# Masked attention weights: transposed by one DMA in place of TensorE and ScalarE

## The chip, the cores and the metric

The kernel runs on 1 core of a Trainium2 chip. The metric is the device time of one execution in microseconds; before the change its median over 3 runs is 1413.26 us (1412.77 to 1415.63). The engines are called as the profile calls them: PE (TensorE, matmuls; PEld its weight loads), DVE (VectorE), ACT (ScalarE), POOL (GpSimd) and SP (SyncE, which here only issues DMAs).

## The reference

Attention over 8 batches of 8 heads, 576 rows of 64 columns, in which each query row keeps its 32 largest scores, followed by an MLP with a squared ReLU over the 4608 rows of 512 columns:

```python
scores = scale * np.matmul(q, k.transpose(0, 1, 3, 2))
kth = np.partition(scores, -top_k, axis=-1)[..., -top_k:-top_k + 1]   # top_k = 32
scores = np.where(scores >= kth, scores, -1e9)
attn = softmax(scores)
x = (attn @ v), heads side by side: [4608, 512]
out = np.maximum(x @ w_in, 0) ** 2 @ w_out                            # 512 -> 2048 -> 512
```

## The kernel before

The 4608 rows are 36 tiles of 128 (`NT`); of each nine, one joins the last 64 rows of two batches (`parts`). A step `n` handles one tile and one half of its heads, four heads (`G`), so there are 72 steps (`NG`). The order of instructions on every engine is that of the Python program (`manual_schedule`); semaphores between the engines come from the tiles that they read and write.

In step `n`:

- DVE selects: `select_a(n)` (L237 to L250) folds each row's 576 scores and takes the first 8 maxima, `select_b(n)` (L263 to L267) takes three more rounds of 8, and `masks(n)` (L278) makes the weights of the four heads: a score at or over the 32nd maximum keeps its exponential, any other becomes 0. The result `p` is bf16, 128 x 576 a head.
- ACT makes the exponentials `e` of this step in two pairs (`exps`, L256), in the third and the fourth of the step's four slots (`for j in range(G)`, L423).
- PE makes the scores of step `n + 1` (`qk_pair`, L221, in slots 0 and 2), which ACT copies to `s` (L226), and finishes the attention of step `n - 1`: in each slot `p_transpose(n - 1, j)` (L288) transposes one head's weights in five blocks into the PSUM tile `tp`, ACT copies it to SBUF as `pt` in two pieces (L290, L291), and `av(n - 1, j)` (L302) multiplies it with `v`.
- One item of the MLP of earlier rows stands between them in each slot (`todo`): four matmuls into `hp` (L342) with ACT's ReLU and square (L345, L346), or four matmuls into `op` (L355), the fourth of which is followed by ACT's copy (L359) and the store (L361).
- The q, k and v tiles of a later batch are loaded by SP (L190), one a slot, and used four slots later: q and k are transposed by PE into `tp` (L200) and copied by ACT (L202), v is cast by POOL (L196). In the first nine steps the MLP's weights come in the same way, one piece a slot, cast by POOL (L391).

`tp` is one PSUM buffer; the transposes of the weights, of q and k, and of the normalised tile `x` (`norm`, L328, every second step) all take it in turn. `p` has two buffers, `pt` three, `s` two.

At the end (L428) the rest of the MLP's items is spread over the last slots. Then `flags` are reduced (L458); a general path, not taken here, would follow where a fold had dropped a maximum.

Of the kernel before, what the change touches and what calls it, by code (L numbers as in the profile page):

```python
# [14 lines left out]
bf16 = mybir.dt.bfloat16  # L15
i32 = mybir.dt.int32
Act = mybir.ActivationFunctionType
# [112 lines left out]
def kernel(  # L130
# [9 lines left out]
    nc = tc.nc  # L140
    B, H, S, D = q.shape
# [4 lines left out]
    G = 4  # L146
    NG = NT * 2
# [7 lines left out]
    with ExitStack() as main:  # L155
        cst = main.enter_context(tc.tile_pool(name="cst", bufs=1))
        sb = main.enter_context(tc.tile_pool(name="sb", bufs=1))
        psp = main.enter_context(tc.tile_pool(name="psp", bufs=1, space=PSUM))
# [3 lines left out]
        idb = cst.tile([128, 128], bf16, name="idb")  # L162
# [5 lines left out]
        def parts(t):  # L168
            b0, r = 2 * (t // 9), t % 9
            if r < 4:  # L170
                return [(b0, r * 128, 128, 0)]
            if r == 4:
                return [(b0, 512, 64, 0), (b0 + 1, 512, 64, 64)]
            return [(b0 + 1, (r - 5) * 128, 128, 0)]
# [34 lines left out]
        s_t, p_t, e_t, sums_t, av_t, xT_t = {}, {}, {}, {}, {}, {}  # L209
# [60 lines left out]

        def masks(n):
            t, hg = n // 2, n % 2
            p_t[n] = sb.tile([128, G, S], bf16, name="p", bufs=2)
            if hg == 0:
                sums_t[t] = sb.tile([128, 8], f32, name="sums", bufs=2)
            for j in range(G):
                h = hg * G + j
                nc.vector.scalar_tensor_tensor(out=p_t[n][:, j, :], in0=s_t[n][:, j, :],  # L278
                                               scalar=m8_t[n][0][:, 3, j, 7:8], in1=e_t[n][:, j, :],
                                               op0=Alu.is_ge, op1=Alu.mult, accum_out=sums_t[t][:, h:h + 1])  # L280

        pt_t = {}

        def p_transpose(n, j):
            tp = psp.tile([128, 5, 128], bf16, name="tp")
            for c in range(5):
                kn = 128 if c < 4 else 64
                nc.tensor.transpose(tp[:kn, c, :], p_t[n][:, j, c * 128:c * 128 + kn], idb[:, :])  # L288
            pt = sb.tile([128, 5, 128], bf16, name="pt", bufs=3)
            nc.scalar.activation(pt[:, :4, :], tp[:, :4, :], Act.Copy)  # L290
            nc.scalar.activation(pt[:64, 4, :], tp[:64, 4, :], Act.Copy)  # L291
            pt_t[n, j] = pt

        def av(n, j):
            t, h = n // 2, (n % 2) * G + j
            if h == 0:
                av_t[t] = psp.tile([128, 8, 64], f32, name="av")
            pt = pt_t.pop((n, j))
            for (b, q0, ql, p0) in parts(t):
                for c in range(5):  # L300
                    kn = 128 if c < 4 else 64
                    nc.tensor.matmul(out=av_t[t][p0:p0 + ql, h, :], lhsT=pt[:kn, c, p0:p0 + ql],  # L302
                                     rhs=vb[b][:kn, c, h * 64:(h + 1) * 64], start=(c == 0), stop=(c == 4))


# [101 lines left out]

        begin = {1: 0}
        for b in range(2, 8):
            begin[b] = (9 * (b // 2 - 1) + 5) * 2 if b % 2 == 0 else 18 * (b // 2)  # L410
        begin_step = {}
        for b, st in begin.items():
            begin_step.setdefault(st, []).append(b)
# [2 lines left out]
        for n in range(NG + 2):  # L416
            for b in begin_step.get(n, []):
                loads += start_load(b)
            if n >= 3 and n % 2 == 1:
                norm((n - 3) // 2)  # L420
            if n < NG:
                select_a(n)
            for j in range(G):  # L423
                if 1 <= n <= NG:
                    p_transpose(n - 1, j)
                if n + 1 < NG and j in (0, 2):
                    qk_pair(n + 1, j // 2)
                take = 1 if n < NG - 2 else -(-len(todo) // max(1, (NG + 1 - n) * G - j)) if n >= NG else -(-len(todo) // max(1, (NG - n) * G - j))  # L428
                for _ in range(take):
                    if todo:  # L430
                        todo.pop(0)()
                if 1 <= n <= NG:
                    av(n - 1, j)
                if n < NG:
                    if j == 2:
                        exps(n, 0)
                        exps(n, 1)
                    if j == 3:
                        exps(n, 2)
                        exps(n, 3)  # L440
                if inflight:
                    inflight.pop(0)()
                while loads and len(inflight) < 4:
                    inflight.append(loads.pop(0)())
                if n < 9 and wq:
                    w_piece()
            if n < NG:
                select_b(n)
                masks(n)
        while todo:  # L450
            todo.pop(0)()


    with ExitStack() as tail:
        sb = tail.enter_context(tc.tile_pool(name="tsb", bufs=1))
# [44 lines left out]
```

## Time and profile before

| | |
|---|---|
| median of 3 runs | 1413.26 us (1412.77 to 1415.63) |
| the profiled execution | 1413.52 us |
| its span in the profile | 1411.7 us |
| DVE busy | 1276.8 us |
| PE busy | 899.7 us |
| ACT busy | 821.5 us |
| POOL busy | 60.7 us |
| mean granted clock of PE | 0.793 of full speed |

The profile is that of one execution. The busy time of an engine is an average over the start (loads), 72 steps and the end (the last MLP items). The page's slices are 35.3 us each. What ended an engine's idle time is named behind `<-`: the line whose instruction came last before it could start. A matmul's end is modelled, so busy PE times are rough.

### The profile page before, as it was taken

Reading aid. Unit: us, or ns where it says so; the run is one execution under the profiler, and the core shown is the slowest. Engines: PE = TensorE matmul, PEld = TensorE weight load, DVE = VectorE, ACT = ScalarE, POOL = GpSimd, SP = SyncE. Lnnn points to the kernel's source line nnn. Section 1 sums busy time; section 2 is a strip of 40 time slices with the busy share of each in tenths; the row PEclk is TensorE's granted clock in tenths of the full one; section 3 lists DMA queues with packets and bytes.
Section 4 is the critical chain, followed back from the end, with each engine's and each line's share of the span. In section 5 each row is a group of like instructions: output and inputs, shape, how many; then the busy total and the mean of one; then the engine's idle time right before and its main releaser. Section 6 shows DMA issues by size and latency. Waiting matters only on the chain.

```text
span 1411.7 us, 19221 instructions
## 1 busy us (share of the span) xinstructions
PE 899.7 (64%) x5914; PEld 500.1 (35%) x6002; DVE 1276.8 (90%) x4828; ACT 821.5 (58%) x1625; POOL 60.7 (4%) x78
## 2 busy tenths in 40 slices
PE   5755566666656667566666667657665666766775
PEld 3433233333333334333333334333333333433333
DVE  4999998999999999999999999989999899999920
ACT  3545466556655567557755675557655664566563
POOL 1240001000100000000000000100010000000000
PEclk9556588877888878887888878867788887878896
DMA  7560001002200200120010002200021000000000
GB/s 172 135 174 16 1 8 38 8 16 64 46 1 16 72 1 16 46 51 21 16 45 11 6 1 49 72 12 1 24 63 45 1 1 16 16 1 1 23 30 10
DMA packets 122478, 47.44 MB, mean 34 GB/s; under 512 B 113664, under 2 KB 113664, under 8 KB 122368
## 3 DMA queue, kind: packets, MB, share of 16 engines
q1 hardware_dynamic: 122368, 46.15, 12.8%
q8 instruction: 48, 0.79, 0.2%
q14 instruction: 62, 0.51, 0.1%
HBM read 36.70 MB, written 9.44 MB: 33 GB/s over the span
## 4 chain that ended last, share of the span: by engine, by line
DVE 61%; PE 21%; ACT 15%; issue 2%; DMA 0%; DVEq 0%; ACTq 0%
DVE p L278 13%; DVE W L263 12%; DVE m L266 9%; PE sc L221 6%; DVE W L242 5%; PE hp L342 4%; DVE m L238 4%; DVE M L237 4%; PE tp L288 4%; ACT e L256 4%; DVE W L245 4%; PE op L355 3%; DVE m L248 3%; ACT r L345 3%; DVE W L239 2%; DVE Mm L240 2%
## 5 line engine op out<-in xcount | busy, mean ns | idle before, releaser
L278 DVE SCALAR_TENSOR_TENSOR p<-s,m,e 128x576 bf16<-128x576 f32 x288 | 225.6, 832 | 72.8 <-ACT e L256 72.5
L263 DVE MATCH_REPLACE8 W<-m,W 128x168 f32<-128x168 f32 x864 | 264.7, 318 | 0.0
L288 PE MATMUL tp<-idb,p 128*128 128x128 bf16 (+1 forms) x1440 | 182.6, 245 | 125.7 <-ACT qT L202 44.3
L290 ACT ACTIVATE pt<-tp 128x512 bf16<-128x512 bf16 x288 | 169.8, 590 | 148.4 <-PE tp L288 147.7
L221 PE MATMUL sc<-kT,qT 64*128 64x288 f32 (+1 forms) x1280 | 244.6, 557 | 1.6 <-ACT s L226 0.9
L226 ACT ACTIVATE s<-sc 128x576 f32<-128x576 f32 x288 | 171.6, 648 | 117.0 <-PE sc L221 109.4
L266 DVE MAX8 m<-W 128x8 f32<-128x168 f32 x864 | 222.4, 320 | 0.0
L256 ACT ACTIVATE e<-s,neg 128x576 bf16<-128x576 f32 x288 | 206.1, 765 | 18.9 <-DVE neg L250 18.4
L302 PE MATMUL av<-vb,pt 128*128 128x64 bf16 (+3 forms) x1600 | 141.2, 204 | 84.0 <-ACT pt L290 81.2
L342 PE MATMUL hp<-xT,wi 128*128 128x512 bf16 (+2 forms) x597 | 166.6, 398 | 29.5 <-ACT r L345 22.1
L288 PEld LDWEIGHTS <-p 128*128 128x128 bf16 (+1 forms) x1440 | 115.2, 108 | 188.0 <-issue 126.7
L302 PEld LDWEIGHTS <-pt 128*128 128x128 bf16 (+3 forms) x1600 | 105.2, 104 | 211.0 <-ACT pt L290 132.3
L328 PE MATMUL tp<-idb,x 128*128 128x128 bf16 x144 | 21.9, 307 | 244.2 <-DVE x L319 244.2
L355 PE MATMUL op<-wo,h 128*128 128x512 bf16 x531 | 152.0, 413 | 8.5 <-issue 7.5
L329 ACT ACTIVATE xT<-tp 128x512 bf16<-128x512 bf16 x36 | 21.5, 597 | 211.0 <-PE tp L328 211.0
L221 PEld LDWEIGHTS sc<-kT,qT 64*128 64x128 f32 (+1 forms) x1280 | 125.7, 228 | 43.6 <-issue 4.2
L237 DVE TENSOR_TENSOR M<-s 128x1152 f32<-128x1152 f32 x72 | 97.4, 1353 | 19.1 <-ACT s L226 19.1
L242 DVE MAX8 W<-m 128x8 f32<-128x288 f32 x288 | 110.2, 443 | 0.0
L345 ACT ACTIVATE r<-hp 128x512 f32<-128x512 f32 (+2 forms) x160 | 88.3, 552 | 26.5 <-PE hp L342 25.9
L328 PEld LDWEIGHTS <-x 128*128 128x128 bf16 x144 | 12.4, 131 | 249.4 <-DVE x L319 249.4
L238 DVE TENSOR_TENSOR m<-s 128x1152 f32<-128x1152 f32 x72 | 99.3, 1379 | 0.0
L346 ACT ACTIVATE h<-r 128x512 bf16<-128x512 f32 (+2 forms) x160 | 94.0, 587 | 5.1
(34 smaller groups left out, 827.9 us busy)
## 6 DMA issues: line engine op xcount, KB each, us to landing
raw<-in_k_dram SPq DMA_DIRECT2D x32, 256.0 KB, 3.7
raw<-in_q_dram SPq DMA_DIRECT2D x32, 256.0 KB, 3.8
raw<-in_v_dram SPq DMA_DIRECT2D x32, 256.0 KB, 3.7
out_dram<-o SPq DMA_DIRECT2D x32, 256.0 KB, 2.1
raw<-in_moe_w_in_dram SPq DMA_DIRECT2D x16, 256.0 KB, 3.8
raw<-in_moe_w_out_dram SPq DMA_DIRECT2D x16, 256.0 KB, 3.4
raw<-in_k_dram SPq DMA_DIRECT2D x8, 128.0 KB, 4.2
raw<-in_v_dram SPq DMA_DIRECT2D x8, 128.0 KB, 2.8
```

Source lines behind the costliest of these rows:

```text
L221: nc.tensor.matmul(out=tiles[o][p0:p0 + ql, half, :HS], lhsT=qT[b][rows, hp, q0:q0 + ql], rhs=kT[b][rows, hp, half * HS:(half + 1) * HS], ...
L226: nc.scalar.activation(s_t[n][:, pair * 2 + o, :].rearrange("p (a c) -> p a c", a=2), tiles[o][:, :, :HS], Act.Copy, scale=scale)
L242: nc.vector.max(out=W[:, j, QS:QS + 8], in_=m[:, j, :])
L256: nc.scalar.activation(e_t[n][:, j, :], s_t[n][:, j, :], Act.Exp, bias=m8_t[n][1][:, j:j + 1])
L263: nc.vector.match_replace(out=W2[:, j, :], in_to_replace=m8[:, r - 1, j, :], in_values=(W if r == 1 else W2)[:, j, :], imm_value=NEG)
L266: nc.vector.max(out=m8[:, r, j, :], in_=W2[:, j, :])
L278: nc.vector.scalar_tensor_tensor(out=p_t[n][:, j, :], in0=s_t[n][:, j, :], scalar=m8_t[n][0][:, 3, j, 7:8], in1=e_t[n][:, j, :], op0=Alu.i ...
L288: nc.tensor.transpose(tp[:kn, c, :], p_t[n][:, j, c * 128:c * 128 + kn], idb[:, :])
L290: nc.scalar.activation(pt[:, :4, :], tp[:, :4, :], Act.Copy)
L302: nc.tensor.matmul(out=av_t[t][p0:p0 + ql, h, :], lhsT=pt[:kn, c, p0:p0 + ql], rhs=vb[b][:kn, c, h * 64:(h + 1) * 64], start=(c == 0), sto ...
L342: nc.tensor.matmul(out=hp[:, :N], lhsT=wi[:, kc, dc * 128:(dc + 1) * 128], rhs=xT[:, kc, :N], start=(kc == 0), stop=(kc == 3))
L355: nc.tensor.matmul(out=op[:, :], lhsT=h2[:, dc, u * 128:(u + 1) * 128], rhs=wo[:, dc, :], start=(dc == 0), stop=(dc == 15))
```

## The change

The two buffers of `p` become fixed tiles of 4 x 640 columns a partition, whose last 64 columns a head are set to 0 once. After the four masks of a step, SP issues one transposing DMA from SBUF to SBUF: 128 partitions x 2560 columns become 20 blocks of 128 x 128, five a head, in `pt`, which now has two buffers of 20 blocks. The transposes on PE, the PSUM tile that they filled and their evacuation by ACT are gone. The sums `av` of the four heads of step `n - 1` move from one a slot to two in each of the last two slots of step `n`. The loading of a batch begins one step later.

```diff
         def masks(n):
-            p_t[n] = sb.tile([128, G, S], bf16, name="p", bufs=2)
+            p_t[n] = p_bufs[n % 2]
...
-                nc.vector.scalar_tensor_tensor(out=p_t[n][:, j, :], in0=s_t[n][:, j, :],
+                nc.vector.scalar_tensor_tensor(out=p_t[n][:, j, :S], in0=s_t[n][:, j, :],
...
-        def p_transpose(n, j):
-            tp = psp.tile([128, 5, 128], bf16, name="tp")
-            for c in range(5):
-                kn = 128 if c < 4 else 64
-                nc.tensor.transpose(tp[:kn, c, :], p_t[n][:, j, c * 128:c * 128 + kn], idb[:, :])
-            pt = sb.tile([128, 5, 128], bf16, name="pt", bufs=3)
-            nc.scalar.activation(pt[:, :4, :], tp[:, :4, :], Act.Copy)
-            nc.scalar.activation(pt[:64, 4, :], tp[:64, 4, :], Act.Copy)
-            pt_t[n, j] = pt
+        p_bufs = [cst.tile([128, G, 640], bf16, name=f"p{i}") for i in range(2)]
+        for pb in p_bufs:
+            nc.gpsimd.memset(pb[:, :, S:], 0.0)
+
+        def p_transpose(n):
+            pt = sb.tile([128, G * 5, 128], bf16, name="pt", bufs=2)
+            nc.sync.dma_start_transpose(out=pt[:, :, :], in_=p_t[n][:, :, :].rearrange("p g k -> p (g k)"))
+            pt_t[n] = pt
 
         def av(n, j):
...
-            pt = pt_t.pop((n, j))
+            pt = pt_t[n]
...
-                    nc.tensor.matmul(out=av_t[t][p0:p0 + ql, h, :], lhsT=pt[:kn, c, p0:p0 + ql],
+                    nc.tensor.matmul(out=av_t[t][p0:p0 + ql, h, :], lhsT=pt[:kn, j * 5 + c, p0:p0 + ql],
...
-            begin[b] = (9 * (b // 2 - 1) + 5) * 2 if b % 2 == 0 else 18 * (b // 2)
+            begin[b] = (9 * (b // 2 - 1) + 5) * 2 + 1 if b % 2 == 0 else 18 * (b // 2) + 1
...
             for j in range(G):
-                if 1 <= n <= NG:
-                    p_transpose(n - 1, j)
                 if n + 1 < NG and j in (0, 2):
                     qk_pair(n + 1, j // 2)
...
-                if 1 <= n <= NG:
-                    av(n - 1, j)
+                if 1 <= n <= NG and j >= 2:
+                    av(n - 1, 2 * j - 4)
+                    av(n - 1, 2 * j - 3)
...
                 select_b(n)
                 masks(n)
+                p_transpose(n)
```

On ACT, this is the second half of step 49 in the kernel before (a step with an MLP item and a q tile in each slot). `sc` are scores, `hp` an MLP item, `e` the exponentials, L202 the evacuation of a q tile:

```order
L226 ACTIVATE s<-sc 128x576 x2
L345 ACTIVATE r<-hp 128x512
L346 ACTIVATE h_8972<-r 128x512
L256 ACTIVATE e<-s,neg 128x576 x2
L202 ACTIVATE qT<-tp 128x4x128
L290 ACTIVATE pt<-tp 128x512
L291 ACTIVATE pt<-tp 64x128
L345 ACTIVATE r<-hp 128x512
L346 ACTIVATE h_8972<-r 128x512
L256 ACTIVATE e<-s,neg 128x576 x2
```

The same place in the kernel after:

```order
L226 ACTIVATE s<-sc 128x576 x2
L343 ACTIVATE r<-hp 128x512
L344 ACTIVATE h_7285<-r 128x512
L256 ACTIVATE e<-s,neg 128x576 x2
L343 ACTIVATE r<-hp 128x512
L344 ACTIVATE h_7285<-r 128x512
L256 ACTIVATE e<-s,neg 128x576 x2
```

Between the two pairs of exponentials stands one MLP item; the evacuations of `pt` are gone, and this step's q tile has moved to a later one with its batch.

On PE, in the same step of the kernel before, the third slot begins behind a q tile (L200), with the transposes of a head, the scores and an MLP item, and ends with that head's sums:

```order
L200 MATMUL tp<-idf,raw 128x128 x4
L288 LDWEIGHTS p
L288 MATMUL tp<-idb,p 128x128
...
L288 MATMUL tp<-idb,p 64x128
L221 MATMUL sc<-kT,qT 128x288 x4
L342 LDWEIGHTS wi
L342 MATMUL hp<-xT,wi 128x512
...
L302 LDWEIGHTS pt
L302 MATMUL av<-vb,pt 128x64
```

The end of that step and the start of the next in the kernel after; the first `av` row is the last of the third slot, and the `av` rows behind the MLP item are ten matmuls, those of two heads:

```order
L300 MATMUL av<-vb,pt 128x64
L340 LDWEIGHTS wi
L340 MATMUL hp<-xT,wi 128x512
...
L300 LDWEIGHTS pt
L300 MATMUL av<-vb,pt 128x64
...
L221 MATMUL sc<-kT,qT 128x288 x4
```

The sums stand in two blocks of two heads, and the fourth slot's MLP item stands behind the first block.

On SP, two steps in which a batch is loaded, after the change (before, the same loads and stores stand one behind the other):

```order
L190 DMA raw<-in_v_dram 128x8x64 [waits DMAHW4_49]
L289 DMA_TRANSPOSE pt<-p_78 128x20x128 [waits DMAHW5_49,DVE_49,PE_49]
L190 DMA raw<-in_v_dram 128x8x64 [waits DMAHW6_49]
L190 DMA raw<-in_v_dram 128x8x64 [waits DMAHW7_49,PE_49]
L190 DMA raw<-in_v_dram 128x8x64 [waits DMAHW0_49,PE_49]
L359 DMA out_dram<-o 128x512 [waits DMAHW1_49,Activation_49]
L190 DMA raw<-in_v_dram 64x8x64 [waits DMAHW2_49,PE_49]
L289 DMA_TRANSPOSE pt<-p_77 128x20x128 [waits DMAHW3_49,DVE_49]
```

The transposing DMA stands behind the step's four loads and its store and waits for DVE, the last mask.

## Rows read from the trace of the kernel before

**Rows 1.** The page: engines' busy time, and DVE in 40 slices (tenths).

```profile
PE 899.7 (64%) x5914; PEld 500.1 (35%) x6002; DVE 1276.8 (90%) x4828; ACT 821.5 (58%) x1625; POOL 60.7 (4%) x78
...
DVE  4999998999999999999999999989999899999920
```

**Rows 2.** The waits of the whole span: us in total, times, longest.

```profile
PE tp L328 <- DVE x L319: 244.2, 36, 8.1
...
DVE p L278 <- ACT e L256: 72.5, 30, 19.3
```

**Rows 3.** The timeline of DVE, two step starts: start us, us, what.

```profile
1005.16 1.35 DVE L237 TENSOR_TENSOR M<-s 128x1152 f32<-128x1152 f32 x1
...
1040.36 1.40 DVE L237 TENSOR_TENSOR M<-s 128x1152 f32<-128x1152 f32 x1
```

**Rows 4.** The timeline of all engines at the end of step 49.

```profile
943.12 1.42 ACT L256 ACTIVATE e<-s,neg 128x576 bf16<-128x576 f32 x2
...
944.46 0.57 ACT L202 ACTIVATE qT<-tp 128x512 f32<-128x512 f32 x1
...
945.08 0.83 PE L288 MATMUL tp<-idb,p 128*128 128x128 bf16 x5 [2.43 <-ACT qT L202]
...
945.84 1.89 PE L342 MATMUL hp<-xT,wi 128*128 128x512 bf16 x4
945.95 0.60 ACT L290 ACTIVATE pt<-tp 128x512 bf16<-128x512 bf16 x1 [0.92 <-PE tp L288]
...
948.93 1.42 ACT L256 ACTIVATE e<-s,neg 128x576 bf16<-128x576 f32 x2
949.73 0.82 DVE L278 SCALAR_TENSOR_TENSOR p<-s,m,e 128x576 bf16<-128x576 f32 x1 [4.24 <-ACT e L256]
```

**Rows 5.** Groups by line, whole span: count, busy us, mean ns, idle before.

```profile
L288 PE MATMUL tp<-idb,p 128*128 128x128 bf16 (+1 forms) x1440 | 182.6, 245 | 125.7 <-ACT qT L202 44.3 <-ACT kT L202 28.8 <-DVE p L278 27.0
...
L290 ACT ACTIVATE pt<-tp 128x512 bf16<-128x512 bf16 x288 | 169.8, 590 | 148.4 <-PE tp L288 147.7
...
L291 ACT ACTIVATE pt<-tp 64x128 bf16<-64x128 bf16 x288 | 74.4, 258 | 0.0
```

**Rows 6.** The page's DMA: queue (packets, MB, share), issues (KB, us to landing).

```profile
q1 hardware_dynamic: 122368, 46.15, 12.8%
...
raw<-in_v_dram SPq DMA_DIRECT2D x32, 256.0 KB, 3.7
out_dram<-o SPq DMA_DIRECT2D x32, 256.0 KB, 2.1
```

**Rows 7.** The timeline of PE in step 50.

```profile
955.93 1.04 PE L342 MATMUL hp<-xT,wi 128*128 128x512 bf16 x4
...
957.08 0.42 PE L302 MATMUL av<-vb,pt 128*128 128x64 bf16 x5
```

**Rows 8.** Windows: length, busy of PE, PEld, DVE, ACT, POOL, clock, DMA, GB/s.

```profile
404.00:412.00 8.00, 0.18 (x3) 0.07 (x1) 7.86 (x34) 2.30 (x4) 0.00 (x0) 0.58 0.00 0
412.00:419.00 7.00, 6.00 (x28) 3.22 (x29) 7.00 (x19) 2.54 (x5) 0.00 (x0) 0.51 0.01 2
```

**Rows 9.** DVE beside a POOL cast, beside DMA (timeline), and the latter's window.

```profile
79.19 1.16 DVE L239 TENSOR_TENSOR W<-M 128x576 f32<-128x576 f32 x1
...
373.28 1.34 DVE L238 TENSOR_TENSOR m<-s 128x1152 f32<-128x1152 f32 x1
374.55 0.75 DVE L239 TENSOR_TENSOR W<-M 128x576 f32<-128x576 f32 x1
...
373.00:374.00 1.00, 0.61 (x5) 0.42 (x4) 1.00 (x2) 0.33 (x1) 0.00 (x0) 0.50 1.11 252
```

**Rows 10.** The timeline of DVE at the end: last step's waits, last normalisation.

```profile
1366.18 0.82 DVE L278 SCALAR_TENSOR_TENSOR p<-s,m,e 128x576 bf16<-128x576 f32 x1 [19.28 <-ACT e L256]
...
1374.84 0.82 DVE L278 SCALAR_TENSOR_TENSOR p<-s,m,e 128x576 bf16<-128x576 f32 x1 [7.09 <-ACT e L256]
...
1382.23 0.69 DVE L319 TENSOR_TENSOR x<-av,rc 128x512 bf16<-128x512 f32 x1 [5.59 <-PE av L302]
```

## The prediction

> **What bounds the kernel now.** I read the shares of the span first. VectorE (DVE) is busy for 1276.8 of 1411.7 us, and its slices read 9 from the second to the thirty-eighth, with an 8 here and there; TensorE (PE) is busy for 899.7 us [rows 1]. So DVE carries the body, and the change, which takes no instruction from DVE, can win only the time in which DVE stands still. The view of waits says what that is: DVE's masking pass waits 30 times for the exponentials of ScalarE (ACT), 72.5 us in all. PE is in the opposite position: 36 times, 244.2 us in all, it waits for DVE's normalised tile [rows 2]. Next the rhythm: DVE starts a step at 1005.16 and the second one after it at 1040.36, so two steps that wait for nothing take 35.20 us, 17.6 us on average (the odd one also normalises) [rows 3].
>
> Two of the 30 waits, 19.28 and 7.09 us, stand in the last step, where the rest of the MLP is pushed between the exponentials [rows 10]. The other 28 make 72.5 - 26.4 = 46.1 us, and they are what the change can reach.
>
> The timeline of the worst step of the body shows where they come from [rows 4]. The weights of a head and the q and k tiles being loaded are transposed through the same single PSUM buffer, tp. In that step ACT first does two exponentials (943.12), then empties tp of a q tile (944.46); PE's transposes of the weights wait 2.43 us for that and start at 945.08; ACT empties them at 945.95, PE does its MLP item, ACT's next exponentials start at 948.93, and DVE, ready for the third mask, has waited 4.24 us by 949.73. It is one loop between PE and ACT, and the transposes of the weights are two links of it in each of a step's four slots.
>
> **The change, part by part.**
>
> *Removed:* 1440 transposes on PE (182.6 us) and 576 evacuations on ACT (169.8 + 74.4 = 244.2 us) [rows 5]. Per step that is 2.5 us of PE and 3.4 us of ACT, besides four handovers each way. Off the DVE path this is worth nothing by itself; its worth is the 46.1 us of waits. In the worst step the wait shown is 4.24 us; the removed ACT work alone is 3.4 us, and the 2.43 us that PE waited for tp go too [rows 4, 5]. I take all 46.1 us as gone. The least it can bring is nothing, the most 46.1 us here.
>
> *Added:* one transposing DMA a step, 128 x 2560 bf16 = 655 KB, issued by SP when the fourth mask is done. No row shows such a DMA. Bounds: a store of 256 KB lands in 2.1 us, a load of 256 KB in 3.7 us, and 2.56 times the latter, all of it scaled with the bytes, is 9.5 us [rows 6]. Between them I count packets. The queue's 122,368 packets took 12.8% of 16 engines x 1411.7 us, so 23.6 ns each [rows 6]. A load is 1024 pieces of 256 B, 64 an engine, 1.5 us, which leaves 2.2 us fixed. If the transpose reads 256 B pieces too (128 columns of one partition), it has 2560, 160 an engine, 3.8 us: T = 6.0 us, an estimate. That is nearest to the load's row, and I take it.
>
> *What waits for T:* the weighted sums (av), which now all stand in the last two slots of the next step. PE runs in order, so behind a late av wait one MLP item and, through ACT, the last two exponentials. From landing to the end of the step: two heads' av (2 x 0.42), the MLP item (1.04 warm, 1.89 at half clock) [rows 4, 7], 1.20 us from that item's end to the exponentials (945.84 + 1.89 = 947.73 to 948.93), half of 1.42 us for the first of them, and two masks, 1.5 us [rows 4]: 5.3 to 6.1 us. So a step of 17.6 us holds T up to about 11.5 us. At 6.0 us the wait is PE's alone, and PE has the room: in the first two slots it has scores and two MLP items to do meanwhile. Even at the bound of 9.5 us DVE would not feel it.
>
> *Moved:* DVE's and POOL's orders stay, but for two small fills of the padding on POOL at the start (hidden at the start, where the engines still wait for the first loads). On SP, the loads and stores of a step now stand behind the transpose that ends the step before, and it behind the fourth mask. Loads are used four slots, a step, after their issue and land in 3.7 us, and stores have no reader: nothing. The start of the batch loads is one step later; the first score that needs such a batch is more than two steps behind its last load: nothing. The masks must find their buffer read by the transpose of two steps before: at T = 6 a step and more of room.
>
> *The end:* in step 71 four heads' transposes leave the PE/ACT chain, about 0.6 us each: -2.4 us. In step 72 the last sums follow the last mask: before, 5.59 us until DVE could normalise [rows 10]; now T plus four av, 6.0 + 4 x 0.5 = 8.0: +2.4 us. Together nothing; at T = 2.1 it is -3.9, at 9.5 it is +3.5.
>
> *Sum:* 1411.7 - 46.1 = 1365.6 us of span. The profiled execution took 1413.52 us, 1.8 more than its span and 0.3 from the median of the runs. So 1367 us. The likeliest case's own range is 1357 to 1382: T at its ends, and up to 12 us of waits left.
>
> **Rivals.**
>
> *1. The transpose lands late (slower).* The place is av, the price T + 5.7 us a step in place of 17.6, and it decides from T = 11.5 us. It needs pieces shorter than the 256 B that I assume: (11.5 - 2.2) us / 23.6 ns is 394 packets an engine, pieces of 104 B. At 64 B it is 640 an engine, 15.1 us, T = 17.3, a step of 23.0 us, and 71 x 5.4 = 383 us more: 1750 us. Two-byte pieces would make 483 us a step, far out of my range. For it: the write side of a transpose scatters, and no row shows one. Against it: the change issues one instruction with the whole tile on both sides, not many small copies. The Trainium skill speaks against the change: its page "VectorE: DVE Perf Modes", in "The three transpose paths", gives 1309 ns for a 128 x 128 block by DMA against 390 ns on TensorE, and its rules advise TensorE where PSUM will do. Twenty blocks one after another would by that be 26 us (an estimate), well past the point; the TensorE figure is not this trace's, which has 245 ns [rows 5], and no row here has the DMA's. Another page, "DMA: Bandwidth & Descriptors", in "Latency and other measured facts", gives 261 GB/s for a transposing DMA, by which 655 KB move in 2.5 us, inside my bounds.
>
> *2. The clock takes half of it back (still faster).* After idle time PE works at the lower level: 404 to 412 us it was nearly idle, and from 412 to 419 us its granted clock is 0.51, the 1.2 GHz level [rows 8]. After the change PE has less to do and idles more, at the step's start and for T. At that level the MLP items take 1.89 us in place of 1.04 [rows 4, 7], four a step, 3.4 us. In steps with loads this could keep half of the waits: 1367 + 23 = 1390 us. Against it: four items at 1.89 us are 7.6 us of a step of 17.6.
>
> *3. The waits are not the transposes' doing (no change).* Loads, MLP items and exponentials alone might make them: 1413 us. Against it, the 2.43 us in the loop [rows 4].
>
> *4. The traffic slows DVE (slower).* The transpose reads and writes SBUF just when DVE makes its first four passes. Beside a POOL cast DVE's W pass took 1.16 us in place of 0.75 [rows 9]. If the DMA did the same to W and Mm, that is 0.82 us a step, 58 us: 1425 us; it decides from 0.65 us a step. Against it: at 373 to 374 us the DMA engines moved 252 GB/s with POOL idle, and the m pass took its usual 1.34 us [rows 9].
>
> **How the numbers follow.** Forecast 0.62; late transpose 0.16; clock 0.11; no change 0.05; slowed DVE 0.06. The time is that of the forecast, 1367 us. The range runs from 1355 us (the forecast's lower end and a little) to 1440 us, over the clock, no change and slowed DVE; it leaves out the late transpose and some tails, 0.19. About 0.2% is what a measurement of this kernel can tell, 2.8 us. Faster is forecast and clock, 0.73; within it, 0.05; slower, late transpose and slowed DVE, 0.22.
>
> **What would show it.** Right: the wait of DVE for ACT's exponentials falls from 72.5 us to some 26, all of it in the last step; DVE's busy time stays within 5 us of 1276.8; PE waits for the DMA at av, many times and a few us each, and ACT's evacuations of pt are gone; the DMA issue lands in 4 to 9 us. Wrong: a landing above 11 us with DVE waiting for the exponentials in nearly every step (rival 1); waits of 1 to 3 us left in steps with loads, at a granted clock near 0.5 (rival 2); M, m, W and Mm longer than 1.35 and 0.75 us without a POOL cast beside them (rival 4).

## The result and the profile after

The kernel after takes 1356.09 us (median of 4 runs, 1356.04 to 1358.32) against 1413.26: a ratio of 0.9596, with a 95% interval of 0.958 to 0.9613. The forecast was 1367. The profiled execution took 1358.32 us, its span is 1356.5, so 55.2 us of span are gone; its mean granted clock is 0.738, where it was 0.793. One run of those reported below, 3130 us in the kernel with five transposes a step, was disturbed and is left out.

The page of the kernel after, against [rows 1]:

```profile
PE 795.8 (59%) x4562; PEld 417.6 (31%) x4562; DVE 1266.3 (93%) x4828; ACT 620.6 (46%) x1049; POOL 45.9 (3%) x80
...
DVE  3999999999999999999999999999999999999910
```

PE and ACT do less, as the change says. DVE has the same 4828 instructions and is busy for 10.5 us less, and its slices have lost their 8s. The waits of the kernel after (total us, times, longest), against [rows 2]:

```profile
PE tp L326 <- DVE x L317: 307.6, 36, 12.3
...
ACT s L226 <- DVE p L278: 162.0, 36, 6.9
...
DVE p L278 <- ACT e L256: 25.4, 2, 18.3
...
PE av L300 <- DMA pt<-p: 8.8, 4, 6.6
```

DVE's 30 waits for the exponentials have become 2, and both stand in the last step (18.32 and 7.08 us, where [rows 10] have 19.28 and 7.09). All 28 waits of the body, 46.1 us, are gone. PE waits for the transposing DMA four times in the whole span. PE's wait for `x` has grown from 244.2 to 307.6 us, which DVE does not feel: none of its own waits in the body is left. One step of the kernel after (timeline, DVE, PE and ACT), against [rows 3, 4]:

```profile
940.18 1.35 DVE L237 TENSOR_TENSOR M<-s 128x1152 f32<-128x1152 f32 x1
...
947.24 0.77 PE L300 MATMUL av<-vb,pt 128*128 128x64 bf16 x10
...
951.08 1.42 ACT L256 ACTIVATE e<-s,neg 128x576 bf16<-128x576 f32 x2
...
954.37 0.81 DVE L278 SCALAR_TENSOR_TENSOR p<-s,m,e 128x576 bf16<-128x576 f32 x1
...
958.24 1.35 DVE L237 TENSOR_TENSOR M<-s 128x1152 f32<-128x1152 f32 x1
```

PE comes to the first sums 7.06 us after the step's start and finds the transpose there. The last exponentials are done at 952.50, before DVE comes to even the first mask at 954.37; in step 49 of the kernel before the third mask stood 4.24 us for them. This step has no q or k tile, though; where one is emptied there is less to spare: in step 50 the last exponentials are done at 918.74 and the first mask starts at 919.16, and in step 19 the last two are done at 373.76 and the last mask starts at 373.87. The transposes in the DMA part of the page, against [rows 6]:

```profile
q1 hardware_dynamic: 308992, 93.34, 29.1%
...
pt<-p SPq DMA_TRANSPOSE x72, 4.1
```

The queue has (308,992 - 122,368) / 72 = 2592 packets a step more. The end of the kernel after (DVE's last normalisation), against [rows 10]:

```profile
1325.39 0.69 DVE L317 TENSOR_TENSOR x<-av,rc 128x512 bf16<-128x512 f32 x1 [6.11 <-PE av L300]
```

From the start of step 71 to the end of the span it is now 80.3 us, before 79.1. The account of the span: 46.1 us of waits, 10.5 us of DVE's busy time, less 1.2 us of a longer end, 55.4 us; 55.2 were measured. Two questions are left: which part of the old path made the waits, and why DVE got faster.

### The profile page after: what moved, and what is told of

It reads as the page before. It is cut to its first block, busy times and chain, and to the rows that moved or that the text cites. A ratio compares the mean times of both kernels' runs of the same rounds, so it can differ in the third digit from the quotient of the medians.

```text
span 1356.5 us, 15960 instructions
## 1 busy us (share of the span) xinstructions
PE 795.8 (59%) x4562; PEld 417.6 (31%) x4562; DVE 1266.3 (93%) x4828; ACT 620.6 (46%) x1049; POOL 45.9 (3%) x80
## 2 busy tenths in 40 slices
DMA packets 309089, 94.45 MB, mean 70 GB/s; under 512 B 300288, under 2 KB 300288, under 8 KB 308992
## 3 DMA queue, kind: packets, MB, share of 16 engines
q1 hardware_dynamic: 308992, 93.34, 29.1%
## 4 chain that ended last, share of the span: by engine, by line
DVE 91%; PE 5%; ACT 2%; issue 1%; DMA 1%; DVEq 0%; ACTq 0%; SPq 0%
DVE W L263 19%; DVE p L278 16%; DVE m L266 15%; DVE W L242 7%; DVE M L237 7%; DVE m L238 7%; DVE W L245 6%; DVE m L248 5%; DVE W L239 3%; DVE Mm L240 3%; PE hp L340 2%; DVE x L317 2%; PE op L353 2%; DVE neg L250 1%; ACT r L343 1%
## 5 line engine op out<-in xcount | busy, mean ns | idle before, releaser
L221 PE MATMUL sc<-kT,qT 64*128 64x288 f32 (+1 forms) x1280 | 271.5, 592 | 48.8 <-ACT s L226 48.1
L263 DVE MATCH_REPLACE8 W<-m,W 128x168 f32<-128x168 f32 x864 | 264.4, 317 | 0.0
L340 PE MATMUL hp<-xT,wi 128*128 128x512 bf16 (+2 forms) x640 | 188.6, 428 | 109.7 <-ACT r L343 108.4
L278 DVE SCALAR_TENSOR_TENSOR p<-s,m,e 128x576 bf16<-128x576 f32 x288 | 220.0, 819 | 25.6 <-ACT e L256 25.4
L326 PE MATMUL tp<-idb,x 128*128 128x128 bf16 x144 | 21.9, 307 | 307.6 <-DVE x L317 307.6
L221 PEld LDWEIGHTS sc<-kT,qT 64*128 64x128 f32 (+1 forms) x1280 | 144.9, 247 | 124.6 <-ACT s L226 59.1
L353 PE MATMUL op<-wo,h 128*128 128x512 bf16 x576 | 174.9, 447 | 0.8 <-ACT o L357 0.7
L300 PE MATMUL av<-vb,pt 128*128 128x64 bf16 (+3 forms) x1600 | 133.0, 206 | 8.8 <-DMA pt<-p 8.8
L340 PEld LDWEIGHTS <-wi 128*128 128x128 bf16 x640 | 62.9, 111 | 216.7 <-issue 190.9
L300 PEld LDWEIGHTS <-pt 128*128 128x128 bf16 (+3 forms) x1600 | 102.8, 105 | 81.0 <-issue 17.7
L237 DVE TENSOR_TENSOR M<-s 128x1152 f32<-128x1152 f32 x72 | 97.7, 1356 | 18.8 <-ACT s L226 18.8
L200 PE MATMUL tp<-idf,raw 128*128 128x128 f32 (+1 forms) x320 | 60.7, 325 | 76.5 <-ACT qT L202 44.9
L353 PEld LDWEIGHTS <-h 128*128 128x128 bf16 x576 | 56.6, 110 | 99.6 <-issue 69.1
```

The source lines that it names most:

```text
L221: nc.tensor.matmul(out=tiles[o][p0:p0 + ql, half, :HS], lhsT=qT[b][rows, hp, q0:q0 + ql], rhs=kT[b][rows, hp, half * HS:(half + 1) * HS], ...
L237: nc.vector.tensor_tensor(out=M[:, :, :], in0=s[:, :, :HS], in1=s[:, :, HS:], op=Alu.max)
L263: nc.vector.match_replace(out=W2[:, j, :], in_to_replace=m8[:, r - 1, j, :], in_values=(W if r == 1 else W2)[:, j, :], imm_value=NEG)
L278: nc.vector.scalar_tensor_tensor(out=p_t[n][:, j, :S], in0=s_t[n][:, j, :], scalar=m8_t[n][0][:, 3, j, 7:8], in1=e_t[n][:, j, :], op0=Alu. ...
L340: nc.tensor.matmul(out=hp[:, :N], lhsT=wi[:, kc, dc * 128:(dc + 1) * 128], rhs=xT[:, kc, :N], start=(kc == 0), stop=(kc == 3))
L353: nc.tensor.matmul(out=op[:, :], lhsT=h2[:, dc, u * 128:(u + 1) * 128], rhs=wo[:, dc, :], start=(dc == 0), stop=(dc == 15))
```

## The experiments

Ratios are to runs of the kernel before on the same chip beside each experiment (their medians are 1413.3 to 1416.9 us), with a 95% interval. "Body waits" are DVE's waits for the exponentials outside the last step, "DVE" its busy time, both of the profiled execution. Line numbers shift by a few with each edit.

**Where the waits came from.** My theory was the loop between PE and ACT through the buffer `tp`. In the kernel before, 38.6 of the 46.1 us of waits stand in steps in which ACT also empties `tp` of a q or k tile. Four kernels put parts of the old work back into the kernel after, with a tile of zeros as the source; nothing reads what they produce.

*Both halves: five transposes on PE and two evacuations on ACT in each slot.*

```diff
+        def dummy():
+            tp = psp.tile([128, 5, 128], bf16, name="tp")
+            for c in range(5):
+                kn = 128 if c < 4 else 64
+                nc.tensor.transpose(tp[:kn, c, :], zero[:, c, :kn], idb[:, :])
+            d = sb.tile([128, 5, 128], bf16, name="dmy", bufs=3)
+            nc.scalar.activation(d[:, :4, :], tp[:, :4, :], Act.Copy)
+            nc.scalar.activation(d[:64, 4, :], tp[:64, 4, :], Act.Copy)
...
             for j in range(G):
+                if 1 <= n <= NG:
+                    dummy()
```

> The kernel after, plus in each slot the five transposes on PE into tp and the two evacuations on ACT that the change removed, of a constant tile, into a tile that nothing reads: their work without their data. Theory (the 46 us of waits came from that work in the loop of PE, tp and ACT, not from where the masks or the sums stood): DVE waits for the exponentials again 25 to 55 us in the body, time 1380 to 1412 us. Rival (the waits came from the order, the weighted sums in every slot, and from the transposes' wait for the masks): body waits below 10 us and the time within 10 us of 1356.

1389.46 us (1388.76 to 1391.09), ratio 0.9808 [0.9784, 0.9832], DVE 1268.7. The waits are back:

```profile
DVE p L278 <- ACT e L256: 54.5, 24, 19.5
```

Less the last step's two, this is 27.6 us in 22 waits. So the old work alone makes more than half of the 46.1 us, although its results go nowhere.

*ACT's half alone: the two evacuations, read from the tile of zeros, without transposes.*

```diff
+            d = sb.tile([128, 5, 128], bf16, name="dmy", bufs=3)
+            nc.scalar.activation(d[:, :4, :], zero[:, :4, :], Act.Copy)
+            nc.scalar.activation(d[:64, 4, :], zero[:64, 4, :], Act.Copy)
```

> The kernel after, plus in each slot only the two evacuations on ACT (a constant tile copied to a tile that nothing reads): 244 us of ACT work, no PE work. Theory (the waits come from the loop in which PE waits for tp, ACT for PE and PE for pt again, so that both halves are needed): body waits for the exponentials below 10 us, time 1356 to 1366 us. Rival (ACT's load alone makes them): body waits 20 to 35 us as with both halves, time 1378 to 1392 us.

1358.64 us (1357.68 to 1359.2), ratio 0.9609 [0.9585, 0.9634], DVE 1266.2:

```profile
DVE p L278 <- ACT e L256: 26.3, 2, 19.2
```

No wait in the body. ACT carries its whole old load here, and DVE doesn't notice: ACT's time as such cost nothing.

*PE's half alone: the five transposes into `tp`, without evacuation.*

```diff
+            tp = psp.tile([128, 5, 128], bf16, name="tp")
+            for c in range(5):
+                kn = 128 if c < 4 else 64
+                nc.tensor.transpose(tp[:kn, c, :], zero[:, c, :kn], idb[:, :])
```

> The kernel after, plus in each slot only the five transposes on PE into tp, of a constant tile, not evacuated. Theory (the loop needs both halves): body waits for the exponentials 0 to 12 us, since PE still waits for tp after each q or k tile, time 1356 to 1370 us. Rival (PE's load and its waits for tp alone make them): body waits 20 to 35 us, time 1378 to 1392 us.

1379.9 us (1379.39 to 1384.17), ratio 0.9768 [0.9739, 0.9798], DVE 1267.2, body waits 19.1 us in 11, more than my theory's 0 to 12 and just under the rival's 20. All of them stand in steps in which a q or k tile is emptied. The waits of this kernel:

```profile
PE tp L299 <- ACT qT L202: 52.2, 30, 3.9
...
DVE p L278 <- ACT e L256: 46.5, 13, 20.0
...
PE tp L299 <- ACT kT L202: 36.4, 35, 2.1
```

PE stands 88.6 us before the dummy transposes until ACT has emptied `tp` of a q or k tile; PE runs in order, so scores and MLP items behind them come late, and with them ACT's exponentials, as in this step (timeline):

```profile
376.58 0.56 PE L299 MATMUL tp<-idb,zero 128*128 128x128 bf16 x5 [2.08 <-ACT kT L202]
377.07 1.89 PE L349 MATMUL hp<-xT,wi 128*128 128x512 bf16 x4
...
379.00 0.60 ACT L352 ACTIVATE r<-hp 128x512 f32<-128x512 f32 x1 [2.46 <-PE hp L349]
...
380.95 0.82 DVE L278 SCALAR_TENSOR_TENSOR p<-s,m,e 128x576 bf16<-128x576 f32 x1 [3.97 <-ACT e L256]
```

This can be the wait or PE's time itself, hence the next one.

*The same PE work without `tp`: the five matmuls write the unused columns of the score banks.*

```diff
+            for c in range(5):
+                kn = 128 if c < 4 else 64
+                nc.tensor.matmul(out=last_sc[0][:kn, c % 2, 320:448], lhsT=zero[:, c, :kn], rhs=idb[:, :],
+                                 start=True, stop=True)
```

> As the run with only the five PE transposes a slot, but the same five 128-column matmuls write a free part of the scores' PSUM banks in place of tp, so they wait for no evacuation; nobody reads them. Theory (the waits come from the wait for tp: there PE waited 88 us for ACT to empty q and k tiles before these transposes, and 19 us of body waits came back): body waits for the exponentials 0 to 5 us, time 1356 to 1362 us. Rival (PE's busy time alone makes them): body waits 14 to 24 us as there, time 1375 to 1385 us.

1356.82 us (1356.13 to 1357.53), ratio 0.9589 [0.9573, 0.9604], DVE 1264.8:

```profile
DVE p L280 <- ACT e L258: 25.4, 2, 17.9
...
PE tp L200 <- ACT qT L202: 6.2, 2, 4.7
...
PE sc L300 <- ACT s L227: 117.1, 47, 5.0
```

No body wait, so PE's time is free as well. But the expectation that these matmuls wait for no evacuation was wrong: PE stands 117.1 us before them (L300), until ACT has emptied the score banks, longer than before `tp`. What differs is where: 112 of these 117 us lie in the first 3 us of a step, where PE has room, while of the 88.6 us before `tp` some 67 us lie later in the step, as in the one above. So neither PE's time nor every wait of PE costs; the wait for `tp` behind a q or k tile does, and I read the difference as one of place. By ablation: 0 us for either engine's work alone, 19.1 us for the transposes' place in the queue for `tp`, 27.6 us when ACT's evacuations of it are added. Both engines' work together without `tp` was not run, so whether the last 8.5 us come from `tp` or from the two loads together is open.

**Where DVE's 10.5 us came from.** The groups by line of the kernel before (count | busy us, mean ns | idle before):

```profile
L278 DVE SCALAR_TENSOR_TENSOR p<-s,m,e 128x576 bf16<-128x576 f32 x288 | 225.6, 832 | 72.8 <-ACT e L256 72.5
...
L239 DVE TENSOR_TENSOR W<-M 128x576 f32<-128x576 f32 x72 | 56.9, 790 | 0.0
...
L196 POOL CAST vb<-raw 128x512 bf16<-128x512 f32 (+1 forms) x40 | 35.1, 897 | 952.7 <-PE av L302 571.5 <-DMA raw<-in_v_dram 381.1
```

and of the kernel after:

```profile
L278 DVE SCALAR_TENSOR_TENSOR p<-s,m,e 128x576 bf16<-128x576 f32 x288 | 220.0, 819 | 25.6 <-ACT e L256 25.4
...
L239 DVE TENSOR_TENSOR W<-M 128x576 f32<-128x576 f32 x72 | 54.1, 751 | 0.0
...
L196 POOL CAST vb<-raw 128x512 bf16<-128x512 f32 (+1 forms) x40 | 25.3, 635 | 861.8 <-DMA raw<-in_v_dram 861.8
```

The passes with two inputs in SBUF (above all L278 and L237 to L240) lost the time, and the v casts of POOL went from 897 to 635 ns. In the kernel before, casts come in a row, across the masks and the next step's folds (timeline):

```profile
367.65 4.49 POOL L196 CAST vb<-raw 128x512 bf16<-128x512 f32 x5 [146.78 <-PE av L302]
...
367.80 1.15 DVE L278 SCALAR_TENSOR_TENSOR p<-s,m,e 128x576 bf16<-128x576 f32 x1
```

A mask takes 1.15 us there instead of 0.81. In the kernel after, a step with v loads looks like this (timeline of SP's queue, POOL and DVE):

```profile
374.61 1.35 DVE L237 TENSOR_TENSOR M<-s 128x1152 f32<-128x1152 f32 x1
374.76 2.60 SPq L289 DMA_TRANSPOSE pt<-p  x1
...
377.40 3.64 SPq L190 DMA_DIRECT2D raw<-in_v_dram  x4
381.13 0.61 POOL L196 CAST vb<-raw 128x512 bf16<-128x512 f32 x1 [11.60 <-DMA raw<-in_v_dram]
...
382.64 0.31 DVE L263 MATCH_REPLACE8 W<-m,W 128x168 f32<-128x168 f32 x1
```

The transpose holds SP until the fourth mask is done, and for 2.60 us more; the loads behind it are issued 2.8 us after the step's start, and the first cast comes 6.5 us after it, beside the selection (MAX8, MATCH_REPLACE8), whose times don't change (L263 317 ns, 318 before). I tested this theory, that it is what SP holds back and not the traffic, from both sides.

*The kernel before with a small DMA on SP that waits for the fourth mask.*

```diff
                 masks(n)
+                gate = sb.tile([128, 8], bf16, name="gate", bufs=2)
+                nc.sync.dma_start(out=gate[:, :], in_=p_t[n][:, 3, :8])
```

> The kernel before, plus one small DMA (128 x 8 of the last mask's output to a scratch tile) that SP issues at each step's end, behind the fourth mask, where the change puts its transposing DMA. Nothing reads the scratch tile. Theory: the 10.5 us by which DVE's busy time fell (1276.8 to 1266.3 us) come from SP being held at each step's end: loads are issued at the step's start and POOL's casts land beside DVE's single-input passes, no longer beside its two-input ones. Then here DVE is busy for 1264 to 1270 us, its waits for the exponentials stay at 65 to 80 us, and the time is about 1403 us. Rival (the batch loads' later start, or the lighter PE and ACT, made DVE's passes shorter): DVE stays at 1275 to 1279 us and the time within 3 us of 1413.

1412.49 us (1409.74 to 1418.68, 12 runs), ratio 0.9977 [0.996, 0.9993], body waits 47.7 us in 28, DVE 1272.1. Not quite half of the effect on DVE came (4.7 us), between theory and rival, and the total moved by 0.2%. A step of it with v loads (timeline):

```profile
555.57 0.47 SPq L451 DMA_DIRECT2D gate<-p  x1
556.14 2.17 SPq L190 DMA_DIRECT2D raw<-in_v_dram  x3
556.37 1.35 DVE L237 TENSOR_TENSOR M<-s 128x1152 f32<-128x1152 f32 x1
...
559.33 2.45 POOL L196 CAST vb<-raw 128x512 bf16<-128x512 f32 x3 [5.88 <-DMA raw<-in_v_dram]
559.57 1.16 DVE L240 TENSOR_TENSOR Mm<-M 128x576 f32<-128x576 f32 x1
```

The small DMA holds the queue for 0.47 us only. So the loads come about 3 us earlier in the step than in the kernel after, and the casts, which begin 3.0 us after the step's start and not 6.5, meet the last fold: 1.16 us in place of 0.75. SP's wait alone takes most casts off the masks (821 ns on average, 819 in the kernel after, 832 before). The folds are not clear (`Mm` 798 ns, 751 after); for that, I conclude, it takes the 2.6 us as well for which the transposing DMA holds the queue.

*The kernel before, with the batches' loads one step later.*

```diff
-            begin[b] = (9 * (b // 2 - 1) + 5) * 2 if b % 2 == 0 else 18 * (b // 2)
+            begin[b] = (9 * (b // 2 - 1) + 5) * 2 + 1 if b % 2 == 0 else 18 * (b // 2) + 1
```

> The kernel before, with the start of each batch's loads one step later and nothing else. Theory (SP's hold makes the casts move): DVE busy stays at 1274 to 1279 us, waits for the exponentials 65 to 80 us, time within 4 us of 1413. Rival (the later start moves the casts, since POOL no longer waits for the last weighted sums of the batch before, 571.5 us in 4 waits): DVE busy at 1266 to 1270 us and the time at about 1403 us.

1397.91 us (1396.48 to 1399.25), ratio 0.9864 [0.9844, 0.9884], DVE 1273.8, body waits 35.3 us in 27. My theory was wrong here: the shift that I had put down as nothing is worth 1.4% in the kernel before, 10.8 us of it in waits and 3.0 us in DVE's busy time.

*Both edits in the kernel before.*

> The kernel before with both side effects and no transposing DMA: the small DMA that holds SP at each step's end, and the later start of the loads. Theory (the two side effects give DVE 4.7 and 3.0 us of the 10.5 and add up, and the later start takes 11 us of the waits): DVE busy 1267 to 1270 us, waits for the exponentials 58 to 66 us, time about 1393 us (1388 to 1399). Rival (they do not add up): DVE busy 1271 us or more and 1397 us or more.

1403.06 us (1400.66 to 1404.05), ratio 0.9913 [0.9898, 0.9928], DVE 1269.5, body waits 42.6 us in 29. DVE's two gains add up (4.7 and 3.0 us apart, 7.3 together); the waits don't follow: with the gate, most of what the later start took away is back. Why is not settled. What is left of the 10.5 us, 3.2 us, is not in these two side effects.

*The kernel after with the old start.*

```diff
-            begin[b] = (9 * (b // 2 - 1) + 5) * 2 + 1 if b % 2 == 0 else 18 * (b // 2) + 1
+            begin[b] = (9 * (b // 2 - 1) + 5) * 2 if b % 2 == 0 else 18 * (b // 2)
```

> The kernel after with the batch loads begun where they began before the change. Theory (the transposing DMA removes the body waits by itself, the later start only moves the v casts): no body waits for the exponentials; POOL waits for the weighted sums again; some casts fall beside the masks, DVE busy 1268 to 1272 us, time 1357 to 1363 us. Rival (the later start is needed, since with the kernel before it alone took 11 us of the waits): 5 to 15 us of body waits and 1362 to 1375 us.

1356.77 us (1355.89 to 1357.99), ratio 0.9589 [0.9576, 0.9603], DVE 1264.2, body waits 0.3 us in 1. So the later start gives the kernel after nothing. The v casts wait for the old sums here (473.6 us in 4 waits), and DVE's gain is whole all the same.

*The kernel after without the transposing DMA.* The sums read a fixed tile of zeros, so the attention part of the output is left out.

```diff
         def p_transpose(n):
-            pt = sb.tile([128, G * 5, 128], bf16, name="pt", bufs=2)
-            nc.sync.dma_start_transpose(out=pt[:, :, :], in_=p_t[n][:, :, :].rearrange("p g k -> p (g k)"))
-            pt_t[n] = pt
+            pt_t[n] = fixed
```

> The kernel after without its transposing DMA: the weighted sums read one fixed tile of zeros, so the output's attention part is left out. Nothing holds SP at a step's end. Both theories: no wait for the exponentials in the body (25 us in the last step). Theory of SP's hold: DVE's busy time goes back up to 1272 to 1277 us; the end is some 4 us shorter (no landing), so 1358 to 1364 us. Rival (later start of the loads, or lighter PE and ACT): DVE stays at 1265 to 1268 us and the time falls to 1350 to 1353 us. A third theory, that the DMA's traffic slows DVE, would show as DVE busy below 1264 us.

1357.42 us (1355.4 to 1357.62), ratio 0.9577 [0.9557, 0.9597], body waits 0. Its page, and its groups by line:

```profile
PE 783.5 (58%) x4497; PEld 417.6 (31%) x4562; DVE 1275.6 (94%) x4828; ACT 620.4 (46%) x1049; POOL 66.2 (5%) x81
```

```profile
L278 DVE SCALAR_TENSOR_TENSOR p<-s,m,e 128x576 bf16<-128x576 f32 x288 | 223.6, 831 | 24.7 <-ACT e L256 24.7
...
L196 POOL CAST vb<-raw 128x512 bf16<-128x512 f32 (+1 forms) x40 | 37.6, 955 | 919.2 <-DMA raw<-in_v_dram 666.5 <-PE av L301 252.5
```

Without the DMA DVE is busy for 9.3 us more, the masks and the casts are long again. So the DMA's 47 MB of traffic do not slow DVE; what the DMA holds back on SP saved it 9 us. The total is nearly the same because the end is shorter, 71.5 us in place of 80.3; 6.0 of these 8.8 us lie between the last step's first mask and its normalisation, which waits for no transpose here.

Over the kernels, the time in which POOL casts while DVE is in a pass with two inputs in SBUF (L237 to L240, L267, L278; worked out from the two timelines) goes with what these passes take in sum, and that with DVE's busy time:

| kernel | casts beside such passes, us | these passes, us | DVE busy, us |
|---|---|---|---|
| after without the DMA | 43.7 | 561.9 | 1275.6 |
| before | 41.8 | 562.0 | 1276.8 |
| before, later start | 38.8 | 560.1 | 1273.8 |
| before, gate | 23.9 | 557.8 | 1272.1 |
| before, gate and later start | 17.7 | 555.1 | 1269.5 |
| PE's half in after | 11.3 | 553.5 | 1267.2 |
| after, old start | 5.5 | 551.0 | 1264.2 |
| after | 5.1 | 551.5 | 1266.3 |

The passes are 10.5 us shorter in the kernel after, the whole of DVE's gain. Of the 41.8 us before, 13.6 are casts of the MLP's weights in the first nine steps, 0.5 after.

**How late the transpose may land.** The DMA is issued three or five times a step, the copies ahead of the real one into a scratch tile.

```diff
+            for _ in range(2):
+                junk = sb.tile([128, G * 5, 128], bf16, name="junk", bufs=2)
+                nc.sync.dma_start_transpose(out=junk[:, :, :], in_=p_t[n][:, :, :].rearrange("p g k -> p (g k)"))
             nc.sync.dma_start_transpose(out=pt[:, :, :], in_=p_t[n][:, :, :].rearrange("p g k -> p (g k)"))
```

*Three times.*

> The kernel after with the transposing DMA issued three times a step, the first two into a scratch tile that nothing reads. One issue holds SP for 2.5 us and lands 4.1 us after its start, so the one that is read lands at about 5.1 + 4.1 = 9.2 us. Theory (a step has room up to about 11.5 us): no body waits for the exponentials, only the end is some 5 us longer: 1358 to 1364 us; PE waits for the DMA in most steps, by about 2 to 4 us. Rival (the traffic, three times 47 MB, or the loads held behind SP slow the body): DVE busy above 1275 us, or body waits, and 1370 us or more.

1393.07 us (1392.37 to 1393.3), ratio 0.985 [0.9825, 0.9875], DVE 1275.4, body waits 23.1 us in 17, all but 0.8 us of it in steps in which a q or k tile is emptied. A step of it in which DVE does not wait (timeline):

```profile
930.71 1.35 DVE L237 TENSOR_TENSOR M<-s 128x1152 f32<-128x1152 f32 x1
...
936.14 2.59 SPq L292 DMA_TRANSPOSE pt<-p  x1
...
940.38 0.92 PE L303 MATMUL av<-vb,pt 128*128 128x64 bf16 x10 [3.82 <-DMA pt<-p]
```

The sums start 9.67 us after the step, in place of 7.06. I had expected next to nothing below T = 11.5 us. In steps without q and k tiles that held; in steps with them PE's and ACT's chain has less room, and the loads, now issued some 5 us later, are cast beside two-input passes again (26.3 us of such casts, these passes 558.0 us, DVE +9.1).

*Five times.*

> The same with five issues a step: the one that is read lands at about 4 x 2.55 + 4.1 = 14.3 us, past the room of about 11.5 us. Theory: a step takes 14.3 + 5.7 = 20.0 us in place of 17.6, DVE waits for the exponentials some 2.4 us in nearly every step, and the time is about 1530 us (1470 to 1600). Rival (the room is larger than worked out, since PE runs ahead of the sums): below 1400 us.

1673.45 us (1671.59 to 1674.3), ratio 1.1831 [1.179, 1.1871], DVE 1285.6, body waits 279.2 us in 71:

```profile
939.06 1.35 DVE L237 TENSOR_TENSOR M<-s 128x1152 f32<-128x1152 f32 x1
...
949.68 2.62 SPq L292 DMA_TRANSPOSE pt<-p  x1
...
954.31 1.05 PE L303 MATMUL av<-vb,pt 128*128 128x64 bf16 x10 [10.18 <-DMA pt<-p]
...
959.18 0.82 DVE L278 SCALAR_TENSOR_TENSOR p<-s,m,e 128x576 bf16<-128x576 f32 x1 [4.17 <-ACT e L256]
...
961.57 1.35 DVE L237 TENSOR_TENSOR M<-s 128x1152 f32<-128x1152 f32 x1
```

This is the mechanism of the first rival in the prediction, in 65 of 71 steps. In the step shown the sums start 15.25 us after the step's start. With T counted from there to the landing (both worked out from the timeline), the 49 steps in which no q or k tile is emptied take T + 6.5 us on average (14.7 and 21.2), the 21 others T + 8.8 (15.2 and 23.9), where I had T + 5.7. So a step of 17.6 us holds T up to about 11.1 us without such a tile and 8.8 us with one, not 11.5. That fits the three issues, which land 9.5 us after a step's start on average: waits in the steps with tiles, next to none in the others. The kernel after, at 4.1, is far from both.

**The end.** The last MLP items are spread over the last slots [rows 10]; here they are spread only over the slots behind the last step.

```diff
-                take = 1 if n < NG - 2 else -(-len(todo) // max(1, (NG + 1 - n) * G - j)) if n >= NG else -(-len(todo) // max(1, (NG - n) * G - j))
+                take = 1 if n < NG else -(-len(todo) // max(1, (NG + 1 - n) * G - j)) if n >= NG else -(-len(todo) // max(1, (NG - n) * G - j))
```

> The kernel after, with the MLP's remaining items taken one a slot up to the last step of the selection, and the rest spread over the two steps behind it (before, they were pushed between the last two steps' exponentials). A version that could beat both. Theory: the waits of 18.3 and 7.1 us for the exponentials in the last step go, the last landing, sums and normalisation lie beside MLP items, and the 7 to 8 us that PE stands still there are won: 1346 to 1351 us. Rival (the end is the MLP's own chain of PE and ACT, whose length does not change): 1354 to 1359 us.

1354.61 us (1352.92 to 1355.32), ratio 0.9569 [0.9555, 0.9583]; no wait for the exponentials is left even in the last step. Waits of DVE, and PE at the end (timeline):

```profile
DVE x L317 <- PE av L300: 31.7, 1, 31.7
...
DVE fm L456 <- PE op L353: 20.9, 1, 20.9
```

```profile
1302.59 0.81 PE L340 MATMUL hp<-xT,wi 128*128 128x384 bf16 x4 [0.58 <-ACT r L343]
...
1303.98 0.81 PE L340 MATMUL hp<-xT,wi 128*128 128x384 bf16 x4 [0.58 <-ACT r L343]
```

The 25 us of waits moved to the normalisation: the end is bound by the MLP items themselves, one every 1.39 us, each waiting for ACT to empty `hp`. Its interval overlaps that of the kernel after, so it is not shown to be better.

## Why the prediction was right, and where it wasn't

**The sign and the main term** were right: the body's waits of 46.1 us went, all 28 of them. That 19.1 us of them hang on the wait for `tp` is shown: the same work on PE without `tp`, or on ACT without it, costs nothing. With ACT's evacuations through `tp` it is 27.6 us. The other 18.5 us are not apportioned. In the kernel before the later start takes 10.8 us, but with the gate beside it the two take only 3.5, and the step from there (42.6 us) to the kernel after with both halves (27.6) changes three things at once: where the sums stand, that the transposes no longer wait for the masks, and how long SP is held.

**That the time falls inside the range** is luck. The terms reach from 1363 us (T at 2.1: 1367 less 3.9) upwards; the recorded lower ends of 1357 and 1355 have no term behind them, and the measured 1356.09 lies between the two.

**"DVE's busy time stays within 5 us of 1276.8"** was wrong: it fell by 10.5 us, and that less 1.2 us at the end is the error (a span of 1365.6 us predicted, 1356.5 measured). The step that failed is the one on what is moved: "the loads and stores of a step now stand behind the transpose ... nothing". I asked only whether a load could come too late, not what else a later landing moves. It moves POOL's casts away from the passes that they lengthen: 41.8 us beside them before, 5.1 after. The row was there: I had used the 1.16 us of a fold beside a cast [rows 9] for a rival that slows DVE, and never asked how much of that is in the kernel before. The Trainium skill has the rule on its page "SBUF — State Buffer", in "Who interferes with whom": a DVE instruction with two SBUF inputs contends with a GpSimd instruction that reads SBUF, one with at most one doesn't, outside the modes that use two ports. The trace agrees: 0.75 to 1.16 us for the fold, 318 and 317 ns for MATCH_REPLACE8. One pass with a single input, `neg`, is longer beside a cast (below); whether it runs in such a mode no run shows. The same part says that a DMA contends with no compute engine, and the kernel without the DMA agrees: M and W take 1.35 and 0.75 us without a cast beside them there, as in the kernel after.

**T** was mis-sized: 6.0 us estimated, 4.1 measured, inside the bounds of 2.1 and 9.5. The count of 256 B pieces was right: 2560 predicted, 2592 seen (32 of them of 4 B). What was too large is the sum around it. Of the transpose issued at 1117.46 us the first packet starts 1.2 us after the issue, the last ends at 3.6, and it lands at 4.1: 2.4 us of moving in place of 3.8, and some 1.6 us fixed in place of 2.2. A packet takes 18.4 ns in place of 23.6 (the queue's share of 16 engines x 1356.5 us, less before's, over 186,624 packets); 162 of them one behind another would be 3.0 us, so an engine's packets partly overlap. The Trainium skill's 1309 ns for one block (page "VectorE: DVE Perf Modes", in "The three transpose paths") does not hold here block after block: 20 blocks landed in 4.1 us, not in the 26 estimated from it. The Trainium skill's 261 GB/s ("DMA: Bandwidth & Descriptors", in "Latency and other measured facts", where it stands for a non-contiguous middle dimension) makes 2.5 us for this tile, an estimate; that is about what the packets take (2.4 us) and what SP's queue is held for (2.55 us).

**"PE waits for the DMA at av, many times and a few us each"** was wrong: four times, 8.8 us. With T at 4.1 us and the first two slots full, PE isn't there before. **The end** was +1.2 us, not 0: the last mask came 1.0 us earlier in its step and not 2.4, the normalisation then waited 0.5 us longer, as the sum gives with T at 4.1, and the part behind it, for which I had no term, grew by 1.7 us. **The room for T** is 11.1 us in steps without q and k tiles and 8.8 with them, not 11.5: the path from the landing to the step's end is 6.5 and 8.8 us, over the upper of my two figures (6.1).

**The rivals.** The late transpose did not come; the kernel with five shows its price where it does. The clock fell indeed (0.793 to 0.738) and cost nothing on DVE's path, since no body wait is left. "No change" is ruled out by the waits. The traffic does not slow DVE: M, m, W and Mm are 1.36, 1.35, 0.75 and 0.75 us after.

## What to carry to other kernels

A small wait on a loaded path can come from one buffer that two kinds of work share, not from the load of either engine; put each half back alone, and then without the buffer, and it shows. When an edit holds a queue, ask where the work behind it lands, and for how long the queue is held, not only whether it lands in time. And compare the same instruction's duration beside different neighbours: what the kernel before already loses there is a gain that an unrelated change can pick up.

## What was new about the hardware

- A cast on POOL and a two-input pass on DVE lengthen each other: the mask 0.81 to 1.15 us, a fold 0.75 to 1.16, the cast 0.61 alone, 0.897 on average in the kernel before. MAX8 and MATCH_REPLACE8 are not touched, nor is the normalisation (0.69 us beside a cast or not), one of whose inputs lies in PSUM.
- A transposing DMA of 128 x 2560 bf16 from SBUF to SBUF lands in 4.1 us (4.1 to 5.9), in 2592 packets, and holds SP's queue for 2.36 to 3.04 us; three in a row keep 4.2 us each from issue to landing (median), and start 2.6 us apart.
- The tiny `neg` pass (L250), with one input of 128 x 4, takes 169 to 173 ns in every kernel here when no cast is beside it, and up to 632 ns beside one. In the kernel after 11 of 72 stand beside a cast (451 ns on average), before 2, so its average rose from 172 to 213 ns: the casts moved onto it.
